# Spectral mixing and SiLU block on one Trainium2 core: x loads, evictions, filter loads and roundings of the ramp moved to other queues and places

## The chip, the core and the metric

The kernel runs on one core of one Trainium2 chip. The metric is the device time of one execution in microseconds (us). The engines are named as in the profile: PE (TensorE, matrix multiply; PEld is its weight load), DVE (VectorE), ACT (ScalarE), POOL (GpSimd) and SP (SyncE, which here only issues transfers). A name with a q, as SPq, is the queue of that engine, where DMA transfers are issued. Each engine executes its own instructions in the order in which the program emits them.

## What is computed

The input x is 8 x 3008 x 256 in float32. Each of the 256 channels is filtered along its 3008 positions in the frequency domain, and the result goes through a two-layer network with SiLU:

```python
X = np.fft.rfft(x, axis=1)
Y = X * (filt_r + 1j * filt_i)[None, :, :]
y = np.fft.irfft(Y, n=x.shape[1], axis=1)      # (8, 3008, 256)
h = y.reshape(24064, 256) @ w_in               # w_in 256 x 2048
g = h * (1.0 / (1.0 + np.exp(-h)))
out = g @ w_out                                # w_out 2048 x 256
```

The two filters are 1505 x 256 in float32. The weights come in as 64-bit floats and are turned into float32 on the chip.

## The kernel before

**Spectral part.** The transform of length 3008 is split into 47 x 64 and done with small matmuls. For one batch it runs in these pieces, all made by the function `spectral`:

- `load_x(u)`, u = 0 to 7, loads an eighth of x, `sums(u)` (DVE, line 292) adds and subtracts its two halves, and `stage1(u)` (PE, line 309) transforms it into two PSUM banks (`pa`). Two evictions by `evac` bring these to SBUF (`t1`), and two transfers issued by POOL (line 314) write them to a scratch tensor d1 in DRAM.
- `load_t2(g)`, g = 0 to 5, reads d1 back in another order (SP, line 383). `forward(g)` transforms (PE, `pb`, line 394), `multiply(g, k)` applies the filters (DVE, line 406), `add(g, k)` finishes the complex product (lines 414 and 415, on POOL in batch 0).
- `inverse(g)` (PE, `pc`), `even` (ACT) and `rows` (DVE, line 446) do the first half of the inverse transform, and `rows` writes to a second scratch tensor d2. `load_t4` reads that back (SP, line 456), `stage3(g)` ends the inverse (PE, `pd`, line 468), and two `evac` copies put each piece into y.

From batch 2 on, most of x is read in a folded form (`load_fold`, `fold`, `stage1_fold`, `evict_fold`), and `load_x`, `sums`, `stage1` are used for u = 6 and 7 only. Batch 1 uses them for all eight.

**Network.** `hidden(step)` and `project(step)` run 384 steps: 48 token groups times 8 pairs of hidden columns, so that a batch is 48 steps. A step's 14 matmuls with 128 x 128 weights (px, pyz, acc) fill PE, and DVE and ACT make the sums and SiLU between them. Each step has eight rounds.

**The ramp** is the straight code from line 777 on, before the first step. It loads x of batch 0, runs the spectral part of batch 0 up to four of its eight stage 3 pieces, and prepares the weights 0 to 8. Weights go in two functions: `weights(jp)` loads a pair of 64-bit blocks (`raw`, lines 711 and 714, on SP), and `rounded(j)` turns one block into float32 with DVE and ACT alternating (`work`, lines 724 to 732) and POOL multiplying the parts (`w_t`, line 737). After every odd j POOL also makes four sums of weights (shown at line 553). In the loop over groups the order is: forward, loads that belong to the group, multiply, add, the inverse of the group before, and at group 1 the roundings 2 and 3.

`load_filters(first, last)` loads the filters in 16 transfers on SP: the part for groups 0 and 1 before stage 1, the rest (groups 2 to 5) at group 0 of the loop, ahead of the raw weights of `weights(1)`. `evac` alternates between DVE (line 229) and ACT (line 231) by a flag.

**The planner.** Batches 1 to 7 are woven into the steps. `put(step, round, piece)` queues a piece for a step and round, counted from the batch's own first step `at`, so negative numbers lie in the batch before. Pieces are emitted in the order of their times by `until`. What is due before step 0 is emitted ahead of the first hidden step. The output stores (line 679, on SP) are queued in the same list: for the first token group of a batch they are due at steps 10.125 and 10.625 of the batch. The t2 loads of the next batch's groups 0 and 1, at `at - 37`, are due at step 11.0, and the t4 load that belongs to stage 3 piece 4 at step 10.375.

Of the kernel before, what the change touches and what calls it, by code (L numbers as in the profile page):

```python
# [52 lines left out]
B, S, C = 8, 3008, 256  # L53
DFF = 2048
N1, N2 = 47, 64
NS, NG = 24, 6
# [18 lines left out]
def slot_residue(g, bank, j):  # L75

    s = 2 * g + bank
    return (s, 47 - s, s + 12, 35 - s)[j]
# [77 lines left out]
def kernel(  # L156
# [9 lines left out]
    nc = tc.nc  # L166
# [42 lines left out]
    x_all = xpool.tile([128, 2, 2, 2 * C], FP32)  # L209
    x_t = [x_all[:, i] for i in range(2)]  # L210

    def load_filters(first, last):

        for j in (0, 2, 1, 3):
            s0, tau = slot_residue(0, 0, j), (1 if j % 2 == 0 else -1)
            for half in range(2):
                off, t = (s0, tau) if half == 0 else (94 - s0, -tau)
                for k, filt in enumerate((filt_r, filt_i)):
                    nc.sync.dma_start(  # L219
                        out=f_t[k][32 * j + half:32 * j + 32:2].rearrange("p g k c -> p (g k) c")[:, first:last],  # L220
                        in_=bass.AP(tensor=filt.tensor, offset=filt.offset + (off + t * first) * C,
                                    ap=[[94 * C, 16], [t * C, last - first], [1, C]]))

    flip = [0]

    def evac(dst, src):
        flip[0] ^= 1
        if flip[0]:
            nc.vector.tensor_copy(out=dst, in_=src)  # L229
        else:  # L230
            nc.scalar.copy(out=dst, in_=src)

    y = {}
    early = [0]

    def bank(b, name, spare=None):

# [11 lines left out]
    def spectral(b):  # L249
# [3 lines left out]
        xs, us, t2s, banks, prods, halves, t4s = {}, {}, {}, {}, {}, {}, {}  # L253

        def load_x(u):


            queue = nc.sync
            if b == 0:
                queue = (nc.sync, nc.scalar)[u % 2]  # L260
                if u == 0:
                    us["t1"] = gpool.tile([128, 2, 2, 2, C], FP32, name="t1_g", tag="g")
                if u in (0, 2):
                    xs["y"] = ypool.tile([128, 2, HALF], FP32, name=f"x_{b}_{u}", tag="y")
                if u < 4:
                    xs[u] = xs["y"][:, u % 2, 0:1024].rearrange("p (a n) -> p a n", a=2)
                elif u < 6:
                    xs[u] = t4pool.tile([128, 2, 2 * C], FP32, name=f"x_{b}_{u}", tag="t4")
                else:
                    xs[u] = x_t[u % 2]  # L270
                (nc.vector, nc.gpsimd)[u % 2].memset(xs[u][32:64], 0.0)
            else:
                xs[u] = x_t[u % 2]

            for r0 in range(3):
                for h in (range(2) if u % 2 == 0 else (1, 0)):
                    queue.dma_start(  # L277
                        out=xs[u][64 * h + r0:64 * h + N1:3],
                        in_=bass.AP(tensor=x.tensor,
                                    offset=x.offset + (b * S + 32 * r0 + 4 * u + 2 * h) * C,  # L280
                                    ap=[[3 * 32 * C, (N1 + 2 - r0) // 3], [32 * N1 * C, 2], [1, 2 * C]]))

        def sums(u):
            if b > 0 or u % 3 == 0:
# [174 lines left out]
        def stage3(g):  # L459
# [17 lines left out]
            for h in range(2):  # L477
# [4 lines left out]
                    load_t2=load_t2, forward=forward, multiply=multiply, add=add, inverse=inverse, even=even, rows=rows, load_t4=load_t4, stage3=stage3)  # L482
# [3 lines left out]
    def put(step, rnd, piece, *args):  # L486

        pending.append((step + rnd / ROUNDS, len(pending), lambda: piece(*args)))

    def plan(b, part):  # L490

        at = STEPS * b

        if b == 1:
            put(at - 51, 0, part["load_x"], 0)
            put(at - 51, 0, part["load_x"], 1)
            for u in range(8):
                put(at + u - (48 if u else 49), 5, part["sums"], u)
                put(at + u - 47, 3, part["stage1"], u)
        else:  # L500
            put(at - 72, 0, part["reverse_x"])
            for f, step, load, places in ((0, -56, -66, ((-60, 3), (-60, 5), (-59, 5), (-58, 5))),
                                          (1, -48, -55, ((-52, 3), (-52, 5), (-51, 5), (-50, 5))),
                                          (2, -40, -44, ((-42, 5), (-41, 3), (-41, 5), (-40, 3)))):
                put(at + load, 0, part["load_fold"], f)
                for k, (fold_step, rnd) in enumerate(places):
                    put(at + fold_step, rnd, part["fold"], f, k)

                put(at + step, 7, part["stage1_fold"], f)
                put(at + step, 7, part["evict_fold"], f, 0)  # L510
                put(at + step + 1, 0, part["evict_fold"], f, 1)
                put(at + step + 1, 5, part["evict_fold"], f, 2)
                put(at + step + 1, 5, part["evict_fold"], f, 3)
            for u, step in ((6, -46), (7, -45)):
                put(at - 47, 0, part["load_x"], u)
                put(at + step, 5, part["sums"], u)
                put(at + step + 1, 3, part["stage1"], u)
        put(at - 37, 0, part["load_t2"], 0)
        put(at - 37, 0, part["load_t2"], 1)
        for g, places in enumerate((  # L520
# [6 lines left out]
            pieces = (("forward", g), ("multiply", g, 0), ("multiply", g, 1), ("add", g, 0), ("add", g, 1))  # L527
            for (step, rnd), (piece, *args) in zip(places, pieces):
                put(at + step, rnd, part[piece], *args)
        for g, step in ((0, -32), (2, -24), (4, -16)):  # L530
            put(at + step, 7, part["inverse"], g, 2)
            put(at + step, 7, part["even"], g, 0, 2)
            put(at + step + 1, 0, part["even"], g, 1, 2)
            put(at + step + 1, 5, part["rows"], g, 0, 2)
            put(at + step + 2, 3, part["rows"], g, 1, 2)
        put(at - 14, 5, part["load_t4"], 0)
        put(at - 14, 5, part["load_t4"], 1)
        for g, step in enumerate((-11, -9, -6, -3)):
            put(at + step, 3, part["stage3"], g)
        plan_rest(b, part)  # L540

    def plan_rest(b, part):

        for g, (step, rnd) in enumerate(((10, 3), (11, 3), (16, 3), (18, 6))):
            put(STEPS * b + step, rnd, part["stage3"], 4 + g)
# [197 lines left out]
    def load_exact(j):  # L743
        for k in range(2):
            nc.sync.dma_start(out=places(j, 0)[:, k],
                              in_=moe_w_in[128 * k:128 * k + 128, 128 * j:128 * j + 128])
            nc.sync.dma_start(out=places(j, 1)[:, k].rearrange("p (q i) -> p q i", q=4),
                              in_=columns(moe_w_out[128 * j:128 * j + 128, :], 1)[:, k])
        if j % 2:
            combine_weights(j // 2)  # L750
# [9 lines left out]
    def weights(jp):  # L760
        if wide:
            load_weights(jp)

    def rounded(j):
        if wide:
            round_weights(j)
        else:
            load_exact(j)

    def inverse_rows(part, g):  # L770
        part["inverse"](g)
        for i in range(2):
            part["even"](g, i)
            part["rows"](g, i)
# [5 lines left out]
    part = spectral(0)  # L780
# [1 line left out]
        part["load_x"](u)  # L782
    nc.sync.dma_start(out=d_t, in_=d_dram.ap())
    weights(0)
    load_filters(0, 4)
    for u in range(3):
        part["sums"](u)
    for u in range(8):
        part["stage1"](u)
        if u + 3 < 8:  # L790
            part["sums"](u + 3)
    part["load_t2"](0)
    part["load_t2"](1)
    nc.sync.dma_start(out=e_t, in_=e_dram.ap())
# [2 lines left out]
    for g in range(NG):  # L797
        part["forward"](g)
        if g == 0:
            load_filters(4, 2 * NG)  # L800
            nc.sync.dma_start(out=wi_t, in_=wi_dram.ap())
            nc.sync.dma_start(out=wq_t, in_=wq_dram.ap())
        if g < 3:
            weights(1 + g)
        for k in range(2):
            part["multiply"](g, k)
        for k in range(2):
            part["add"](g, k)
        if g > 0:
            inverse_rows(part, g - 1)  # L810
        if g == 1:
            rounded(2)
            rounded(3)
    inverse_rows(part, NG - 1)
    weights(4)
    part["load_t4"](0)
# [78 lines left out]
```

## Time and profile before

| | value |
|---|---|
| time, median of 3 runs | 2656.36 us (2656.26 to 2659.49) |
| the profiled execution | 2659.17 us, span 2657.4 us |
| mean granted PE clock | 0.985 |
| PE busy in 0:20, 20:40, 40:60, 60:80, 80:100, 100:120, 120:140 us | 8.0, 8.8, 11.6, 2.1, 14.7, 6.7, 11.1 us of 20 |
| share of the DMA engines in the same stretches | 0.54, 0.92, 0.78, 0.87, 0.63, 0.69, 0.41 |
| x issues of batch 0 | SP 2.07 to 20.55 us, ACT 0.91 to 21.65 us |
| last write of d1 issued by POOL | 34.83 us |
| first matmul of the first step (px, line 582) | 124.84 us |

Times within the execution count from the start of the span. In a line of the timeline the first two numbers are the start and the length in us, then come engine, line, operation, what it writes and reads, and how many instructions were merged. In brackets stands how long the engine was idle before, and what ended that. The ramp ends at about 125 us, and the steps take about 6.55 us each from then on, longer at first.

The chain that ended last, over the whole span, is nearly all PE:

```profile
PE 92%; DVE 2%; SPq 2%; DMA 2%; issue 1%; ACT 0%; POOL 0%; DVEq 0%; ACTq 0%; POOLq 0%
```

### The profile page before, as it was taken

The numbers are of one execution on the slowest core, as the hardware profiler recorded it, in microseconds if no ns is written. First come the engines' busy times: TensorE is split into PE (matmuls) and PEld (weight loads), VectorE is DVE, ScalarE is ACT, GpSimd is POOL, SyncE is SP. The second block draws the span as 40 slices with busy tenths as digits, with TensorE's granted clock in tenths as the row PEclk, the third lists the DMA queues.
The fourth block names the chain that finished last, engine by engine and source line by source line (L and its number), as shares of the span: only waits on it lengthen the run. The fifth ranks groups of instructions, "written<-read, shape, count | busy, mean of one in ns | idle before, by whom it ended". The sixth has DMA issues, their size and how long they took to land.

```text
span 2657.4 us, 48231 instructions
## 1 busy us (share of the span) xinstructions
PE 2559.0 (96%) x18720; PEld 2162.9 (81%) x18720; DVE 1725.0 (65%) x3590; ACT 1096.3 (41%) x3000; POOL 482.7 (18%) x726
## 2 busy tenths in 40 slices
PE   4489999999999999999999999999999999999998
PEld 1268888888888888888888888888888888888987
DVE  4786666667666676666666676666766666555554
ACT  1244444444444444444444444444444444444443
POOL 3441111311121112111211111131112111100100
PEclk9599999999999999999999999999999999999999
DMA  7632222232223212331232222223222321211000
GB/s 214 189 105 64 71 65 57 63 74 72 59 69 70 62 61 71 76 68 42 69 75 62 65 72 64 56 67 71 66 65 69 74 57 28 55 22 21 9 16 16
DMA packets 207275, 176.11 MB, mean 66 GB/s; under 512 B 123812, under 2 KB 178852, under 8 KB 206644
## 3 DMA queue, kind: packets, MB, share of 16 engines
q1 hardware_dynamic: 185952, 120.91, 19.5%
q0 software_dynamic: 17296, 47.47, 5.6%
q10 hardware_dynamic: 3800, 4.67, 0.6%
q8 instruction: 147, 2.41, 0.4%
q14 instruction: 80, 0.66, 0.1%
HBM read 97.97 MB, written 84.41 MB: 69 GB/s over the span
## 4 chain that ended last, share of the span: by engine, by line
PE 92%; DVE 2%; SPq 2%; DMA 2%; issue 1%; ACT 0%; POOL 0%; DVEq 0%; ACTq 0%; POOLq 0%
PE acc L641 42%; PE px L582 25%; PE pyz L582 18%; PE pd L468 2%; PE pb L394 2%; PE pc L427 2%; SPq L277 1%; DMA t<-d 1%; PE pf L364 1%; PE pa L309 1%; DMA raw<-in_moe_w_out_dram 0%; SPq L219 0%; DVE g L553 0%; DVE u L292 0%; SPq L679 0%
## 5 line engine op out<-in xcount | busy, mean ns | idle before, releaser
L641 PE MATMUL acc<-g,w_t 128*128 128x256 f32 (+1 forms) x5376 | 1512.6, 375 | 0.4 <-DVE g L553 0.4
L641 PEld LDWEIGHTS acc<-g,w_t 128*128 128x128 f32 x5376 | 1022.1, 190 | 116.0 <-DVE g L553 0.8
L553 DVE TENSOR_TENSOR g<-pyz,abc 128x256 f32<-128x256 f32 (+1 forms) x1152 | 479.4, 416 | 542.4 <-ACT abc L603 301.3
L553 DVE TENSOR_TENSOR g<-g 128x256 f32<-128x256 f32 (+3 forms) x1152 | 619.4, 538 | 196.8 <-ACT g L586 183.6
L582 PE MATMUL px<-ty,w_t 128*128 128x256 f32 (+1 forms) x2304 | 688.0, 380 | 3.9 <-ACT abc L597 3.4
L586 ACT ACTIVATE g<-g 128x256 f32<-128x256 f32 (+1 forms) x1152 | 472.9, 410 | 247.1 <-DVE g L553 247.1
L553 POOL TENSOR_TENSOR s<-s 128x256 f32<-128x256 f32 (+1 forms) x329 | 259.7, 806 | 1455.8 <-DVE s L659 1444.8
L582 PEld LDWEIGHTS px<-ty,w_t 128*128 128x128 f32 x2304 | 424.2, 190 | 89.1 <-issue 31.5
L582 PE MATMUL pyz<-y,w_t 128*128 128x256 f32 (+1 forms) x1536 | 454.6, 378 | 1.7 <-DVE g L553 1.7
L582 PEld LDWEIGHTS pyz<-y,w_t 128*128 128x128 f32 x1536 | 284.1, 190 | 47.7 <-DVE g L553 7.2
L597 ACT COPY abc<-px 128x256 f32<-128x256 f32 (+1 forms) x384 | 141.5, 369 | 366.5 <-PE px L582 366.5
L603 ACT COPY abc<-px 128x256 f32<-128x256 f32 (+1 forms) x384 | 143.9, 375 | 317.3 <-PE px L582 317.0
L586 ACT ACTIVATE g<-px 128x256 f32<-128x256 f32 (+1 forms) x384 | 146.1, 380 | 307.7 <-PE px L582 307.7
L582 PE MATMUL px<-y,w_t 128*128 128x256 f32 (+1 forms) x768 | 230.6, 382 | 3.6 <-ACT g L586 2.7
L582 PE MATMUL pyz<-ty,w_t 128*128 128x256 f32 (+1 forms) x768 | 225.8, 376 | 5.0 <-DVE g L553 5.0
L582 PEld LDWEIGHTS px<-y,w_t 128*128 128x128 f32 x768 | 142.3, 190 | 43.0 <-ACT g L586 15.4
L582 PEld LDWEIGHTS pyz<-ty,w_t 128*128 128x128 f32 x768 | 145.9, 190 | 22.5 <-DVE g L553 6.2
L590 ACT COPY abc<-px 128x256 f32<-128x256 f32 (+1 forms) x384 | 135.3, 352 | 2.7 <-PE px L582 1.3
L229 DVE COPY y<-pd 128x376 f32<-128x376 f32 x64 | 51.2, 805 | 98.4 <-PE pd L468 98.4
L394 PE MATMUL pb<-t,d_t 64*32 64x256 f32 x1536 | 63.0, 407 | 38.8 <-DVE p L406 20.4
L468 PEld LDWEIGHTS pd<-wi_t,t 48*64 48x64 f32 x4096 | 69.4, 140 | 36.9 <-issue 25.1
L468 PE MATMUL pd<-wi_t,t 48*64 48x47 f32 x4096 | 77.6, 239 | 16.1 <-issue 8.4
(67 smaller groups left out, 1339.4 us busy)
## 6 DMA issues: line engine op xcount, KB each, us to landing
t<-d SPq DMA_DIRECT2D x96, 256.0 KB
t<-d SPq DMA_DIRECT2D x128, 192.0 KB
d<-q POOLq DMA_DIRECT2D x85, 256.0 KB, 2.6
out_dram<-o SPq DMA_DIRECT2D x636, 32.0 KB
d<-tf POOLq DMA_DIRECT2D x144, 96.0 KB, 2.6
d<-t POOLq DMA_DIRECT2D x52, 192.0 KB, 3.1
xr<-in_x_dram SPq DMA_DIRECT2D x6, 1472.0 KB
x_all<-in_x_dram SPq DMA_DIRECT2D x72, 96.0 KB
```

The source lines that it names most:

```text
L229: nc.vector.tensor_copy(out=dst, in_=src)
L277: queue.dma_start(out=xs[u][64 * h + r0:64 * h + N1:3], in_=bass.AP(tensor=x.tensor, offset=x.offset + (b * S + 32 * r0 + 4 * u + 2 * h) * ...
L394: nc.tensor.matmul(out=ps[k][32 * j:32 * j + 32, ri, :], lhsT=d_t[rows, 4 * g + at, ri, :], rhs=t2[rows, at, :], start=True, stop=True)
L427: nc.tensor.matmul(out=ps[j][64 * k:64 * k + 64, a, :], lhsT=e_t[rows, g + a, k, ri, :], rhs=zs[k][rows, ri, :], start=(a == 0 and ri == 0 ...
L468: nc.tensor.matmul(out=ps[h][c0:c0 + 64, cb, i, :], lhsT=t4s[g][rows, i, 128 * cb + c0:128 * cb + c0 + 64], rhs=wi_t[rows, :], start=True, ...
L553: eng.tensor_tensor(out=out, in0=in0, in1=in1, op=op)
L582: nc.tensor.matmul(out=out, lhsT=w_t[:, c, 0, jp], rhs=rhs, start=start, stop=True, skip_group_check=True)
L586: nc.scalar.activation(out=g[:, k, 0:n], in_=g[:, k, 0:n] if src is None else src, func=AFT.Silu)
L590: nc.scalar.copy(out=sums[:, 0, 0:n], in_=xo)
L597: nc.scalar.copy(out=sums[:, 1, 0:n], in_=xo)
L603: nc.scalar.copy(out=sums[:, 2, 0:n], in_=xo)
L641: nc.tensor.matmul(out=acc[pair][i][:, h, 0:n], lhsT=w_t[:, c, 1, jp], rhs=g[:, k, 0:n], start=(jp == 0 and h == 0), stop=last, skip_group ...
```

## The change

It has six edits, four in the ramp and two in the planner:

1. x of batch 0 is issued by SP alone and no longer by SP and ACT in turn (the choice of queue in `load_x` goes). Each u takes four transfers (rows 0 to 31 and 32 to 46 of each half) in place of six (every third row). The four-transfer form also holds for the later batches.
2. `evac` uses ACT alone as long as the ramp lasts (`early[0]` becomes None at its end), and alternates after it.
3. The second part of the filters is issued by POOL, after stage 1, and no longer by SP at group 0.
4. The rounding of weights 3 moves from group 1 to group 3.
5. The ahead-of-step-0 exception for `sums(0)` of batch 1 goes: it is due one step later, at step 0.625.
6. The t2 loads of groups 0 and 1 of the later batches are due one step earlier, at step 10.0.

```diff
-    def load_filters(first, last):
+    def load_filters(queue, first, last):
...
-                    nc.sync.dma_start(
+                    queue.dma_start(
...
-    flip = [0]
+    flip, early = [0], [0]
     def evac(dst, src):
         flip[0] ^= 1
-        if flip[0]:
+        if flip[0] and early[0] is None:
             nc.vector.tensor_copy(out=dst, in_=src)
         else:
             nc.scalar.copy(out=dst, in_=src)
...
-            queue = nc.sync
             if b == 0:
-                queue = (nc.sync, nc.scalar)[u % 2]
...
-            for r0 in range(3):
-                for h in (range(2) if u % 2 == 0 else (1, 0)):
-                    queue.dma_start(
-                        out=xs[u][64 * h + r0:64 * h + N1:3],
+            for h in range(2):
+                for r0, nr in ((0, 32), (32, N1 - 32)):
+                    nc.sync.dma_start(
+                        out=xs[u][64 * h + r0:64 * h + r0 + nr],
                         in_=bass.AP(tensor=x.tensor,
                                     offset=x.offset + (b * S + 32 * r0 + 4 * u + 2 * h) * C,
-                                    ap=[[3 * 32 * C, (N1 + 2 - r0) // 3], [32 * N1 * C, 2], [1, 2 * C]]))
+                                    ap=[[32 * C, nr], [32 * N1 * C, 2], [1, 2 * C]]))
...
-                put(at + u - (48 if u else 49), 5, part["sums"], u)
+                put(at + u - 48, 5, part["sums"], u)
...
-        put(at - 37, 0, part["load_t2"], 0)
-        put(at - 37, 0, part["load_t2"], 1)
+        put(at - 38, 0, part["load_t2"], 0)
+        put(at - 38, 0, part["load_t2"], 1)
...
-    load_filters(0, 4)
+    load_filters(nc.sync, 0, 4)
...
+    load_filters(nc.gpsimd, 4, 2 * NG)
     part["load_t2"](0)
...
         if g == 0:
-            load_filters(4, 2 * NG)
             nc.sync.dma_start(out=wi_t, in_=wi_dram.ap())
...
-        if g == 1:
-            rounded(2)
-            rounded(3)
+        if g in (1, 3):
+            rounded(2 + g // 2)
```

More of the change, by code (lines that the diff above doesn't have):

```diff
@@ L233 @@
     y = {}
-    early = [0]
     def bank(b, name, spare=None):
```

## The prediction

> **What bounds the kernel now.** I read the page's busy line first, then the table of stretches over the first 200 us, then the waits of each engine in the first 140 us, and last the timeline at the places that these named. All durations below are of the one profiled execution, whose span is 2657.4 us. Its own time is 2659.17 us, and the median of the three timed runs is 2656.36 us, so I carry the difference that I work out over to the median. About 5 us (0.2%) is what a measurement of this kernel can tell from no change.
>
> The page shows TensorE busy nearly throughout, and its slices show where it isn't.
>
> ```profile
> PE 2559.0 (96%) x18720; PEld 2162.9 (81%) x18720; DVE 1725.0 (65%) x3590; ACT 1096.3 (41%) x3000; POOL 482.7 (18%) x726
> ...
> PE   4489999999999999999999999999999999999998
> ```
>
> Each slice is 66 us. After the first two slices TensorE sets the pace, so an edit there pays only where it removes a hole on TensorE itself. In the first 140 us (the ramp: spectral part of batch 0 and the first half of the weights) TensorE is mostly idle, and there the chain runs through DMA, VectorE and the queues. The waits of the ramp, engine by engine (total us, times, longest us):
>
> ```profile
> DVE work L724 <- DMA raw<-in_moe_w_out_dram: 14.6, 1, 14.6
> ...
> DVE u L292 <- DMA x_all<-in_x_dram: 4.7, 1, 4.7
> ...
> PE pb L394 <- DVE p L406: 20.4, 1, 20.4
> ```
>
> VectorE executes in order. It stood 14.6 us for the second block of raw weights, and the multiply of group 2 was queued behind two roundings of those weights, so TensorE stood 20.4 us for the banks. The timeline shows the order (start, length, what):
>
> ```profile
> 40.39 2.78 SPq L383 DMA_DIRECT2D t<-d  x4
> ...
> 48.86 1.44 SPq L219 DMA_DIRECT2D filt<-in_filt_r_dram  x1
> ...
> 64.02 0.59 SPq L219 DMA_DIRECT2D filt<-in_filt_i_dram  x1
> ...
> 66.23 0.47 SPq L714 DMA_DIRECT2D raw<-in_moe_w_out_dram  x1
> ...
> 70.05 0.43 DVE L724 TENSOR_SCALAR work<-raw 128x512 uint32<-128x512 uint32 x1 [14.64 <-DMA raw<-in_moe_w_out_dram]
> ...
> 76.34 0.68 DVE L406 TENSOR_TENSOR z<-pb,filt 128x512 f32<-128x512 f32 x1
> ```
>
> The raw weights wait in SP's order behind the 16 filter transfers, which take SP from 48.86 to 64.6. A smaller hole of this kind lies at the seam to the steady loop, and another recurs once per batch:
>
> ```profile
> 131.09 1.29 DVE L292 TENSOR_TENSOR u<-x_all 111x512 f32<-111x512 f32 x2 [4.65 <-DMA x_all<-in_x_dram]
> 132.30 0.42 DVE L553 TENSOR_TENSOR g<-pyz,abc 128x256 f32<-128x256 f32 x1
> ...
> 132.77 1.22 PE L582 MATMUL pyz<-ty,w_t 128*128 128x256 f32 x2 [5.03 <-DVE g L553]
> ```
> ```profile
> 853.73 4.58 SPq L679 DMA_DIRECT2D out_dram<-o  x8
> 858.66 2.71 SPq L383 DMA_DIRECT2D t<-d  x4
> ...
> 861.55 0.59 PE L641 MATMUL acc<-g,w_t 128*128 128x256 f32 x2
> 862.45 0.59 PE L394 MATMUL pb<-t,d_t 64*32 64x256 f32 x2 [0.31 <-DMA t<-d]
> 864.17 1.09 PE L394 MATMUL pb<-t,d_t 64*32 64x256 f32 x30 [1.13 <-DMA t<-d]
> ```
>
> In the first, VectorE waits for x of batch 1 with the first hidden step's work behind it. In the second, the t2 loads come right after a block of output stores on SP, and TensorE reaches the forward transform before they have landed.
>
> **What the Trainium skill says.** "DMA: Bandwidth & Descriptors", section "Issuing engines are not separate DMA queues": transfers from every issuing engine run on the same 16 DMA engines, and issuing from several saves only sequencer time. The trace agrees: the DMA share is 0.91 to 1.05 from 24 to 36 us with three issuers at work. So I count the moved filter bytes in full. Same page, "Why a DMA increments its semaphore by 16 and not by 1": a transfer is spread over the largest number of engines up to 16 that divides the outer dimensions of both sides. Pieces of 32 and 15 rows give 16 and 15 engines, as 16 and 15 rows do now, so fewer transfers cost no spread. No run here shows that yet.
>
> **Part 1, the x loads and the evictions of stage 1.** Now 48 transfers for batch 0, 24 on SP (2.07 to 20.55) and 24 on ACT (0.91 to 21.65), about 0.78 us each. After, 32 on SP. SP's lone filter issues at 61.5 to 64.6 are 0.64 us apart, and its x issues of batch 1 have a median of 0.63 us, so I take 0.66: SP ends x at about 1.2 + 32 x 0.66 = 22.4 us, 1.8 us later than now (25 if they stay at 0.78, 21 at 0.62). Behind it on SP wait d_t, raw weights and 16 first filter transfers. In exchange ACT issues nothing, so that its first eviction need not wait until 21.69, which now holds the first write of d1 on POOL (16.2 us of wait, 22.58). All 16 evictions at 0.59 us on ACT are 9.4 us and fit beside x, which brings one u each 2.64 us. With 2.2 us to land, the last x is there at 24.7, its sums take 1.3, its matmuls 2.5, the evictions 1.2: d1 is written by about 34 us (now 38 to 39). But the t2 loads follow the first filters on SP, which end at 40.06 now and at 37 to 42 after. Net on the path to the first forward transform: 0, bounds -2 and +2.
>
> **Part 2, the second filters to POOL.** SP loses 16 issues, 15.8 us from 48.86 to 64.6. POOL gets 16 behind the last d1 write, from 30.5 on. POOL's d1 issues are 0.53 us each (8 in 4.27), so 8.5 us, until 39. Queued behind on POOL: the products and sums of weights 0 and 1 (1.66 + 1.42 + 2.88 = 6.0 us, until 45), then the first add, now at 48.91. It stays hidden. What SP issues next after t2 of group 2 (47.58, 1.24 us) is wi, wq and the second raw weights, four transfers in 1.9 us, so they are issued by about 52 and not 67.7. Can the DMA engines follow? Share times length of stretch up to the raw weights' landing at 70 sums to about 50 us of full DMA work. Up to 22 us some 15.5 of it can be done (x about 10.5, five eighths of the 7.7 that d1's 3.07 MB take at the 400 GB/s of 28 to 36 us, so 5). The other 34.5, if the engines then stay full, end at 56.5. I take 57 for the landing, bounds 52 and 63. VectorE is through with rows of group 0 at 55.4, so it waits 1 to 2 us and not 14.6.
>
> **Part 3, the roundings.** Two took 70.05 to 76.34; one is 2.9 to 3.0. So the multiply of group 2 starts at 57.1 + 3.0 = 60.1 and not 76.34: -16.2. The rounding put at group 3 adds its 3.4 us (72.92 to 76.34) there: +3.4, bounds 0 (hidden in VectorE's waits between groups) and +6, if POOL's 1.43 + 2.89 us for it hold the adds of group 4. They held those of group 2 now, so I charge nothing more. The ramp after that (five roundings, 101.48 to 121.07) is VectorE's and moves as a whole.
>
> **Part 4, stage 3's eight evictions on ACT.** Now VectorE takes four, from 120.99 behind the roundings, and the fourth stage 3 piece waits 2.15 us for a bank; the last eviction ends at 124.74. ACT is free at 118.6 and needs 0.70 us each: six by 122.8, the last piece's matmuls from 120.0 + 0.8 to 122.9, its two evictions to 124.3. -0.4, bounds -1.5 and +1.
>
> **Part 5, the first sums of batch 1 one step later.** The add of the first hidden step needs no x; it can run at 127 and not 132.3. The idle taken out is 4.65 us; the sums' own 1.29 us now lie within step 0, where VectorE has gaps of 0.78 and 1.71. By round 5 x is long there, in four transfers and not six. -4.3, bounds -5 and -2.
>
> **Part 6, t2 loads a step (6.55 us) earlier.** They pass ahead of the two blocks of output stores (8 transfers each, 4.2 and 4.6 us) and the t4 load. The last d1 write of batch 3 is issued at 846.19 and takes 2.6 us to land, so SP waits to about 849, and holds the stores by some 4 us; the next use of their buffers is nine steps away. t2 lands near 855, forward comes at 862. I measured from the start of the last acc pair to the next px pair: 3.33, 1.68, 3.64, 2.72, 1.55, 2.50, 1.76 us for batches 1 to 7. Against the 1.55 without a wait that is 1.78 + 0.13 + 2.09 + 1.17 + 0 + 0.95 + 0.21 = 6.3 us. -6.3, bounds -6.3 and 0.
>
> **Sum.** -16.2 + 3.4 - 0.4 - 4.3 - 6.3 = -23.8 us: span 2633.6, time 2656.36 - 23.8, about 2632.5 us.
>
> **The rivals.** *DMA-bound front* (0.24): with x, d1, raw weights and all filters in the first 45 us the t2 loads and raw weights get their turns late, or the rounding at group 3 costs its 6. The multiply of group 2 starts at 66, and the ramp gives -10.3 + 6 = -4.3; with -0.4, -4.3 and -4 from the rest -13: 2643. For it: shares of 1.05. Against it: 0.42 to 0.73 from 52 to 68, so there is room.
>
> *No gain in the ramp* (0.05): another wait of VectorE, for example on the adds of POOL, takes the place of the 14.6 us and only half of parts 5 and 6 remains, -5: 2651.
>
> *Slower* (0.05): POOL's filter issues stall. At p us each, the first add comes at 30.5 + 16p + 6, rows and one rounding follow 11.1 us later, and then 3.4. Parts 4 to 6 give 11 back, so the kernel gets slower once 16p exceeds about 37, p = 2.3 us. At p = 3 it is 2657 + 11, about 2668 us. For it: SP's own filter issues reached 1.88 us under a full DMA. Against it: no POOL issue in this ramp exceeds 0.62.
>
> **How the numbers follow.** The forecast has 0.66, with its own range 2624 to 2640 (landing at 52 to 63, the group 3 rounding at 0 to 6, t2 at half). To leave out no more than 2 in 10 I reach into the first rival: 2622 to 2645. Faster by over 0.2%: 0.92 (both first cases and part of the third); within: 0.04; slower: 0.04.
>
> **What would show it.** Right: the filter issues on POOL take 0.5 to 0.7 us each; the raw weights' wait before L724 shrinks to under 3 us; the multiply of group 2 starts near 60; the first px matmul comes near 111 to 113; VectorE's 4.65 us at the seam and TensorE's waits for t2 vanish. Wrong: the wait before L724 returns as one on POOL or on t2, or the d1 writes still end at 38.

## The result, and the profile after

| | before | after |
|---|---|---|
| time, median of 4 runs | 2656.31 us (2654.53 to 2659.49) | 2637.99 us (2635.87 to 2639.39) |
| ratio after to before | | 0.9929, 95% interval 0.9912 to 0.9946 |
| the profiled execution: time, span | 2659.17, 2657.4 us | 2635.87, 2633.7 us |
| first forward transform (`pb`) | 44.21 us | 45.48 us |
| multiply of group 2 starts | 76.34 | 63.22 |
| rows of the ramp end | 101.57 | 90.08 |
| first matmul of the first step (px) | 124.84 | 112.52 |
| first stage 1 matmul of batch 1 (`pa`) | 142.07 | 124.39 |

The kernel is 18.3 us faster by the medians (0.7%), 23.7 us by the two spans. The predicted 2632.5 us is 5.5 us too low, and the time lies within the range. Line numbers after the change are 3 lower from stage 1 on (line 403 is 406 of before).

The page after, busy time and PE's slices of 66 us: the second slice has gone from 4 to 6, the others stand.

```profile
PE 2559.7 (97%) x18720; PEld 2161.6 (82%) x18720; DVE 1716.9 (65%) x3578; ACT 1101.3 (42%) x3012; POOL 491.7 (19%) x742
...
PE   4689999999999999999999999999999999999998
```

VectorE's waits in the first 140 us after the change (total us, times, longest us):

```profile
DVE z L403 <- PE pb L391: 14.0, 1, 14.0
DVE q L443 <- ACT q L435: 7.8, 7, 2.7
DVE work L721 <- DMA raw<-in_moe_w_out_dram: 5.5, 1, 5.5
```

The 14.6 us for raw weights 2 are gone. The 5.5 us are those of weights 0, early in the ramp, and the 14.0 are the wait for the first forward transform (8.2 before). Of the rest, the seven waits for ACT's copy `q` will matter. TensorE's wait of 20.4 us for the banks of group 2 is gone as well, and its largest wait in the ramp is now the one for t2, which was 13.1 us before:

```profile
PE pb L391 <- DMA t<-d: 20.6, 3, 20.0
```

The timeline after, first the ramp and then the seam to the steps:

```profile
10.27 1.22 POOL L311 DMA_DIRECT2D d<-t  x2 [3.93 <-ACT t L232]
...
27.95 0.51 POOL L219 DMA_DIRECT2D filt<-in_filt_r_dram  x1
...
39.41 0.51 POOL L219 DMA_DIRECT2D filt<-in_filt_i_dram  x1 [0.17 <-issue]
...
53.92 0.47 SPq L711 DMA_DIRECT2D raw<-in_moe_w_out_dram  x1
...
57.72 0.34 ACTq L448 DMA_DIRECT2D d<-q  x1
...
58.51 0.88 DVE L443 TENSOR_TENSOR q<-q,pc 128x256 f32<-128x256 f32 x2 [2.71 <-ACT q L435]
59.30 0.42 DVE L721 TENSOR_SCALAR work<-raw 128x512 uint32<-128x512 uint32 x1
...
63.22 0.68 DVE L403 TENSOR_TENSOR z<-pb,filt 128x512 f32<-128x512 f32 x1
...
115.24 1.16 PE L579 MATMUL pyz<-ty,w_t 128*128 128x256 f32 x2
...
119.05 2.06 DVE L289 TENSOR_TENSOR u<-x_all 111x512 f32<-111x512 f32 x2
```

The first write of d1 is issued at 10.27 and not at 22.58. The filters' second part leaves POOL from 27.95 to 39.9, the raw weights are issued by 54.4 (before 67.7), and the rounding at 59.30 finds them there: no bracket stands behind it. The multiply of group 2 follows at 63.22. At the seam the second pair of pyz matmuls starts within the first step, without the 5.03 us of before, and the sums of batch 1 come after it.

**The difference, step by step.** The differences of the times in the table are -11.5 us at the end of rows, -12.3 at px (so -0.8 from the evictions of stage 3) and -17.7 at `pa` of batch 1 (-5.4 from the seam). Stage 3 piece 4 of batch 0, at 199 us, is still at -17.4 us. From there to the last batch the gap grows to -23.8 in steps of 0.0 to 2.1 us, one at the forward transforms of each later batch, which is -6.3 us. TensorE has no wait for t2 left after 200 us, where before it had six, 3.5 us in all.

### The profile page after: what moved, and what is told of

Its sections match the earlier page's. It is cut to its first block, busy times and chain, and to the rows that moved or that the text cites. A ratio compares the mean times of both kernels' runs of the same rounds, so it can differ in the third digit from the quotient of the medians.

```text
span 2633.7 us, 48160 instructions
## 1 busy us (share of the span) xinstructions
PE 2559.7 (97%) x18720; PEld 2161.6 (82%) x18720; DVE 1716.9 (65%) x3578; ACT 1101.3 (42%) x3012; POOL 491.7 (19%) x742
## 4 chain that ended last, share of the span: by engine, by line
PE 94%; DVE 3%; DMA 1%; issue 1%; ACT 1%; SPq 0%; POOL 0%; ACTq 0%; DVEq 0%; POOLq 0%
PE acc L638 42%; PE px L579 25%; PE pyz L579 18%; PE pd L465 2%; PE pb L391 2%; PE pc L424 2%; PE pf L361 1%; PE pa L306 1%; DVE g L550 1%; DVE u L289 0%; SPq L274 0%; DMA t<-d 0%; DVE work L726 0%; DMA filt<-in_filt_r_dram 0%; DVE work L721 0%
## 5 line engine op out<-in xcount | busy, mean ns | idle before, releaser
L232 ACT COPY y<-pd 128x376 f32<-128x376 f32 x68 | 53.9, 813 | 86.8 <-PE pd L465 86.8
```

## The experiments

In all of them "before" is the kernel before, run on the same chip. px stands for the start of the first px matmul, the end of the ramp. Two profiles of the changed kernel give px 112.52 and 113.79, and the three ramps with none of the ramp's edits (before, t2_alone, sums_alone) 123.5 to 124.8: about 1.3 us is not to be told from nothing in one profile.

| kernel | time us | before us | ratio, 95% interval | px us | multiply of group 2 |
|---|---|---|---|---|---|
| changed_again | 2637.20 | 2658.11 | 0.9922 (0.9910 to 0.9935) | 113.79 | 64.55 |
| t2_alone | 2652.35 | 2657.93 | 0.9977 (0.9970 to 0.9985) | 123.99 | 74.88 |
| sums_alone | 2652.74 | 2657.93 | 0.9980 (0.9972 to 0.9988) | 123.53 | 75.02 |
| f_filters_alone | 2657.13 | 2657.93 | 0.9997 (0.9989 to 1.0006) | 122.58 | 74.20 |
| u_filters_back | 2643.43 | 2657.93 | 0.9944 (0.9930 to 0.9958) | 120.74 | 69.27 |
| u_x_two_queues | 2643.33 | 2658.11 | 0.9942 (0.9927 to 0.9957) | 121.52 | 72.27 |
| u_evac_alternate | 2637.35 | 2658.11 | 0.9921 (0.9907 to 0.9935) | 114.58 | 64.49 |
| u_round_together | 2639.67 | 2658.11 | 0.9929 (0.9916 to 0.9943) | 115.76 | 68.28 |
| m_filters_later | 2643.51 | 2657.49 | 0.9950 (0.9933 to 0.9966) | 118.97 | 69.72 |
| m_filters_act | 2648.59 | 2657.49 | 0.9968 (0.9956 to 0.9979) | 124.99 | 75.71 |
| m_rows_pool | 2633.28 | 2657.49 | 0.9910 (0.9896 to 0.9925) | 111.04 | 61.66 |
| m_rows_pool_t2_first | 2634.65 | 2658.44 | 0.9911 (0.9894 to 0.9927) | 111.16 | 62.85 |

### The two planner edits, each alone

t2_alone is the kernel before with the t2 loads one step earlier:

```diff
-        put(at - 37, 0, part["load_t2"], 0)
-        put(at - 37, 0, part["load_t2"], 1)
+        put(at - 38, 0, part["load_t2"], 0)
+        put(at - 38, 0, part["load_t2"], 1)
```

> The kernel before, with one edit: t2 loads of groups 0 and 1 due at step 10.0. My theory: TensorE's waits at the first forward transform of batches 1 to 7 vanish, 6.3 us in sum; the ramp stays as it is to 0.3 us. Time -6 us (ratio 0.9977). Rival (SP waits for d1 and the output stores behind it come late, so that VectorE's transposes or the t4 load stall): waits of TensorE at pd or at the steps with transposes appear and the time is the same or longer.

Measured: 5.6 us by the medians, 7.3 by the spans, of which 0.85 are already there at px, where nothing was changed. So 6.4 us came from the steps. Each of the seven gaps that the prediction measured is 1.55 us here, and also in the changed kernel. What they hold above that is 6.3 us in the profile of before, but 5.2 and 5.4 us in f_filters_alone and sums_alone, whose t2 loads stand where they stood: the waits differ between executions, and the edit takes all of them. The timeline of t2_alone at the place that the prediction showed of before:

```profile
844.51 3.31 SPq L383 DMA_DIRECT2D t<-d  x4
847.92 4.33 SPq L679 DMA_DIRECT2D out_dram<-o  x8
```

The loads now go first. The output stores behind them are held by about 3 us; the list of waits after 200 us has none for a DMA any more, so nothing waited for them.

sums_alone is the kernel before without the exception for `sums(0)`:

```diff
-                put(at + u - (48 if u else 49), 5, part["sums"], u)
+                put(at + u - 48, 5, part["sums"], u)
```

> The kernel before, with one edit: the first sums of batch 1 are due at step 0.625. My theory: the 4.65 us for which VectorE waits for x ahead of the first hidden step vanish; the sums' own 1.3 us come back within the step in part: -4 to -5.4 us (ratio 0.9982), the first px matmul unchanged at 124.8, the first stage 1 matmul of batch 1 at 137 and not 142.1. Rival (x still late, so the wait only moves within step 0, or later x loads come late and VectorE waits at the next sums): -1 us or less.

Measured: 5.2 us by the medians. `pa` of batch 1 comes 6.4 us earlier and px 1.3 us, so the seam itself gave 5.1 us. Both planner edits came out as expected; they stand alone and need nothing of the ramp.

### The filters on POOL, alone and taken back

f_filters_alone is the kernel before with only the third edit:

```diff
+    load_filters(nc.gpsimd, 4, 2 * NG)
     part["load_t2"](0)
...
         if g == 0:
-            load_filters(4, 2 * NG)
```

> The kernel before, with one edit: the second part of the filters is issued by POOL after stage 1. My theory: the stall of VectorE on the second raw weights goes, since SP issues them some 15 us earlier. d1 is still written by 34.8, so POOL issues the filters until 43 and t2 lands some 3 us later than the 44 of before. Raw weights landed near 60, both roundings follow (6.3 us), the multiply of group 2 starts near 67 and not 76.3, the first px matmul comes at 115 to 116 and not 124.8: about -9.5 us in time. Rival, that the gain of the ramp comes mainly from the x loads and evictions of stage 1: -3 us or less, with the first px matmul after 121.

Measured: 0.8 us by the medians, with an interval that holds no change, and px at 122.58. The theory's 9.5 us did not come; what the rival named did. The timeline of f_filters_alone:

```profile
47.22 1.03 PE L394 MATMUL pb<-t,d_t 64*32 64x256 f32 x2 [16.11 <-DMA t<-d]
...
55.03 1.03 PE L394 MATMUL pb<-t,d_t 64*32 64x256 f32 x2 [2.75 <-DMA t<-d]
...
60.22 2.21 PE L427 MATMUL pc<-z,e_t 32*64 32x256 f32 x32 [1.31 <-DMA e_t<-e_tbl]
...
67.26 0.42 DVE L724 TENSOR_SCALAR work<-raw 128x512 uint32<-128x512 uint32 x1
```

The wait for raw weights 2 is gone here too (the rounding at 67.26 has none), but what stands ahead of it came later. The forward transforms of group 0 began at 47.22 and of group 1 at 55.03 (before, the first at 44.21, with no pause of over 0.3 us for t2 in the next two blocks), and the inverse waited for `e_t` until 60.2. POOL's 16 issues stretched from 35.63 to 48.74 us. So the moved bytes came in the way of t2 and `e_t`.

u_filters_back is the changed kernel with the filters on SP at group 0 again, and every other edit in place:

```diff
-    load_filters(nc.gpsimd, 4, 2 * NG)
     part["load_t2"](0)
...
         if g == 0:
+            load_filters(nc.sync, 4, 2 * NG)
```

> The changed kernel, with the second filters issued by SP at group 0 again. My theory: SP is held for 15 us again ahead of the raw weights, which land near 71; one rounding follows and the multiply of group 2 starts at 74 and not 63, the first px matmul near 123 and not 112.5: some 10 to 11 us slower than the changed kernel, about -13 against the kernel before. The t2 loads land 1 to 2 us earlier than in the changed kernel, since the filters are not in the DMA engines then, and nothing comes of it. Rival (x loads and evictions are the cause): no more than 4 us slower than the changed kernel.

Measured: px 120.74, with the old wait back (12.1 us for raw weights 2). By the gains over before it is 3.8 to 6.4 us slower than the changed kernel, less than the theory's 10 to 11. Against before, the filters alone move px by -2.3 us, everything else in the ramp by -4.1, and all together by -12.3 (-11.1 in the second profile). The two parts make 6.4 of these: about half of the ramp's gain comes only when both are there.

### What the filters need: x off ACT

u_x_two_queues is the changed kernel with `load_x` as before, on SP and ACT in turn and in six transfers:

```diff
+            queue = nc.sync
             if b == 0:
+                queue = (nc.sync, nc.scalar)[u % 2]
...
-            for h in range(2):
-                for r0, nr in ((0, 32), (32, N1 - 32)):
-                    nc.sync.dma_start(
...
+            for r0 in range(3):
+                for h in (range(2) if u % 2 == 0 else (1, 0)):
+                    queue.dma_start(
...
```

> The changed kernel with x loaded as before: SP and ACT in turn, six transfers for each u; evictions stay on ACT. My theory, after seeing that moving the filters alone brought 2 us: the front lives on d1 being written before the filters get into the DMA engines. ACT issues x until 21.7, its 16 evictions end near 31 and not 26.6, the last d1 write near 33.5 and not 28, POOL's filters start there and run into the t2 loads, the multiply of group 2 starts at 67 to 69, the first px matmul at 117 to 119: +5 to +7 us. Rival (the x edit pays nothing, the filters are enough once the rounding is split): first px matmul within 1.5 us of the changed kernel.

Measured: 6.1 us slower than changed_again on the same chip, as the theory had it, though px at 121.52 and the multiply of group 2 at 72.27 come later than it said. Its timeline shows where:

```profile
21.67 4.24 ACT L232 COPY t<-pa 128x512 f32<-128x512 f32 x8 [19.43 <-DMA x_all<-in_x_dram]
...
23.04 4.29 POOL L312 DMA_DIRECT2D d<-t  x8 [16.68 <-ACT t L232]
```

ACT makes no eviction before its own x issues have ended at 21.6, so POOL writes no d1 before 23.04. With x on SP alone the first write goes at 10.27. What that does to the DMA engines is seen in the stretches (columns: stretch, us, busy time of PE, PEld, DVE, ACT and POOL with instructions, granted clock, DMA share, GB/s). First the changed kernel, then f_filters_alone:

```profile
0.00:24.00 24.00, 16.45 (x62) 5.08 (x64) 14.06 (x21) 9.00 (x16) 12.05 (x22) 1.00 0.80 240
24.00:48.00 24.00, 3.54 (x33) 0.87 (x32) 5.00 (x10) 3.56 (x6) 16.02 (x28) 1.00 1.04 289
48.00:76.00 28.00, 20.37 (x278) 8.29 (x262) 19.50 (x39) 4.86 (x11) 12.47 (x19) 0.82 0.89 263
```

```profile
0.00:24.00 24.00, 9.73 (x34) 2.79 (x38) 12.99 (x20) 3.05 (x5) 7.15 (x13) 1.00 0.57 157
24.00:48.00 24.00, 7.89 (x36) 2.22 (x28) 10.57 (x19) 5.42 (x9) 15.29 (x29) 1.00 1.03 303
48.00:76.00 28.00, 12.87 (x161) 5.71 (x160) 14.15 (x26) 3.60 (x7) 14.90 (x22) 0.85 1.08 260
```

Share times length gives the busy time of the DMA engines. By 76 us it is the same in both: 19.2 + 25.0 + 24.9 = 69.1 us and 13.7 + 24.7 + 30.2 = 68.6 us. By 48 us it is 44.2 against 38.4. (Busy time is not bytes: GB/s times length gives 12.7 and 11.0 MB by 48 us, and 20.1 and 18.3 MB by 76.) Before, the three shares were 0.58, 0.92 and 0.77, and in u_x_two_queues 0.59, 1.00 and 1.06. So with x on two queues the engines stood idle for some 10 of the first 24 us, and that time could not be had back once they were full. The x edit fills 5 us of it, with d1 writes above all. The room that this makes is seen in u_filters_back, which has the x edit and not the filters on POOL:

```profile
24.00:48.00 24.00, 6.59 (x65) 2.30 (x72) 8.76 (x16) 3.67 (x6) 8.46 (x13) 1.00 0.73 236
```

From 24 to 48 us 6.5 us of DMA time are free there, and 2 were before. Into this room the filters go. Moved alone they only find full engines.

Edit 1 has two halves, the one queue and the four transfers in place of six. No run parts them, but the lengths of the issues say something (min/median/max in ns): first batch 0 of before, then batch 1 of before, which is on SP alone in the old form, then the first 24 issues of the changed kernel:

```profile
L277 ACTq DMA_DIRECT2D x<-in_x_dram x18: 597/632/1411, 0.9 to 16.2; - x18
L277 SPq DMA_DIRECT2D x<-in_x_dram x18: 592/700/961, 2.1 to 15.2; - x18
...
L277 SPq DMA_DIRECT2D x_all<-in_x_dram x48: 588/628/1475, 124.8 to 185.4; - x48
...
L274 SPq DMA_DIRECT2D x<-in_x_dram x24: 341/380/663, 1.1 to 12.2; - x24
```

An issue of the old form takes about as long on SP alone as beside ACT, and one of the new form is shorter: 0.38 us for these 24, 0.59 for the last eight of batch 0, and 0.43 for batch 1. At 0.63 us each the 48 issues of the old form would hold a lone SP for at least 30 us (an estimate from these lines), where the 32 of the new form took 17.3. So it seems to be the new form that lets SP do x alone. Why its issues are shorter is open.

### Evictions and roundings

u_evac_alternate is the changed kernel with the evictions shared as before:

```diff
-        if flip[0] and early[0] is None:
+        if flip[0]:
```

> The changed kernel with evictions alternating between VectorE and ACT in the ramp again. My theory: ACT is free of x issues, so stage 1 keeps pace with x either way and d1 ends within 0.7 us of 28; at the end of the ramp VectorE's four y copies come after the roundings again: first px matmul +0.5 to +1.5 us. Rival (ACT as the only evictor is what frees the front): +3 us or more.

Measured: 2637.35 us beside changed_again's 2637.20, no difference; px 0.8 us after the one and 2.1 after the other profile of the changed kernel. The stretch from the end of rows to px shows what the edit does: it takes 23.24 to 23.28 us in the five profiles in which VectorE shares the evictions, and 22.35 to 22.44 in the nine others. So it gives 0.9 us at the end of the ramp, too little for the medians to show. The first write of d1 is issued at 12.26, so even here it comes 10 us earlier than before. Freeing ACT of x issues did that, not giving it all evictions.

u_round_together is the changed kernel with both roundings at group 1:

```diff
-        if g in (1, 3):
-            rounded(2 + g // 2)
+        if g == 1:
+            rounded(2)
+            rounded(3)
```

> The changed kernel with roundings 2 and 3 both at group 1. My theory: VectorE's work is the same; the multiply of group 2 starts 3 us later (66.3), and the groups behind it run 1.5 to 3 us shorter: first px matmul 0 to +1.5 us. Rival (the split takes a wait off the path): +3 us or more.

Measured: px 2.0 us after changed_again's. The multiply of group 2 comes 3.7 us later (68.28 against 64.55), and from there to the end of rows it takes 25.1 us, the 25.2 of before; the changed kernel takes 26.9. So splitting the roundings wins 3.7 and costs 1.7. By the medians it is 2.5 us on the same chip, with intervals that overlap; px lies between the theory's 1.5 and the rival's 3 us.

### Who issues the filters, and when

If the filters only have to stay out of the way of t2, they can go later. m_filters_later is the changed kernel with POOL's call behind `rounded(1)`:

```diff
-    load_filters(nc.gpsimd, 4, 2 * NG)
     part["load_t2"](0)
...
     rounded(1)
+    load_filters(nc.gpsimd, 4, 2 * NG)
```

> The changed kernel with POOL's filter issues moved behind POOL's work for weights 0 and 1, ahead of the first adds. My theory is that the filters' bytes in the DMA engines ahead of t2 cost t2 its 3 us: the first forward transform starts at 42.4 to 43.5 and not 45.5 to 46. But POOL's issues (13 us where it has to wait for earlier transfers) now stand ahead of the first adds, so these come at 51 to 55: first px matmul 112 to 116, time the same as the changed kernel or up to 3 us more. Rival (t2 is late for another reason, as the first filters on SP): first forward stays at 45 or later.

Measured: 2643.51 us, px 118.97. The first forward came early as thought, at 42.17, but the gain did not follow. The timeline of m_filters_later:

```profile
54.45 0.51 POOL L219 DMA_DIRECT2D filt<-in_filt_i_dram  x1 [0.24 <-DMA filt<-in_filt_i_dram]
...
55.77 1.11 PE L424 MATMUL pc<-z,e_t 32*64 32x256 f32 x2 [6.29 <-POOL z L411]
```

POOL's issues, from 40.53 to 54.96, stood before its first adds, and the inverse waited for those. The first add came 4.6 us later than in the changed kernel, and the multiply of group 2 6.5 us later. The other 2 us stand at VectorE's wait for ACT's second copy `q`, 4.83 us here and 2.71 in the changed kernel. So the loss is above the theory's 3 us. If the issues stand in the way on POOL, another engine could make them. m_filters_act is m_filters_later with `nc.scalar` in place of `nc.gpsimd`:

```diff
-    load_filters(nc.gpsimd, 4, 2 * NG)
+    load_filters(nc.scalar, 4, 2 * NG)
```

> The changed kernel with the second filters issued by ACT after roundings 0 and 1. My theory: when the bytes go decides and not who issues them. ACT issues from 34 to about 45, where it has nothing else to do until 54; t2 lands at 44 to 46, POOL is free for weights and adds, so the multiply of group 2 starts within 2 us of the changed kernel's 63.2 to 64.6, first px matmul 111 to 114. Rival (POOL's own queue is what makes it work, a queue shared by order with other loads would hold them up): first px matmul after 117.

Measured: 2648.59 us; it is the slowest of the variants that keep every other edit. The timeline of m_filters_act:

```profile
32.83 0.62 ACTq L219 DMA_DIRECT2D filt<-in_filt_r_dram  x1
...
65.23 0.53 ACTq L219 DMA_DIRECT2D filt<-in_filt_i_dram  x1
65.81 0.37 ACT L435 COPY q<-pc 128x256 f32<-128x256 f32 x1 [32.26 <-DMA raw<-in_moe_w_in_dram]
66.21 0.88 DVE L443 TENSOR_TENSOR q<-q,pc 128x256 f32<-128x256 f32 x2 [11.30 <-ACT q L435]
```

Sixteen issues of about 0.6 us each took 33 us. The first six came 0.65 us apart; from 42 to 66 us, where the DMA share is 1.03, up to 8.8 us lie between the starts of two. ACT's next copy stood behind them, and VectorE 11.3 us behind that. "DMA: Bandwidth & Descriptors" of the Trainium skill, section "Issuing engines are not separate DMA queues", says that issuing from another engine saves sequencer time only. No run here contradicts that, as no choice of queue made room in the full stretch. But the engine that issues also pays for the stall, and that is the larger price. Why the same issues ended at 65.8 us on ACT and at 55.0 on POOL is open.

### The same stall, on ACT's d2 writes

The changed kernel has that stall too: ACT's d2 write (57.72 in the timeline above) was issued 1.9 us after its rows had ended, and VectorE stood 2.71 us for ACT's copy at 58.51 and 1.47 us more in the rounding, where it stood 0.84 and 0.42 us before. m_rows_pool is the changed kernel with all d2 writes of the ramp on POOL:

```diff
-                queue = nc.gpsimd if b > 0 or (g == NG - 1 and i == 0) else nc.scalar
-                queue.dma_start(out=d2[a0:a0 + 4].rearrange("a n h c -> (a n) h c"), in_=qt[:, a])
+                nc.gpsimd.dma_start(out=d2[a0:a0 + 4].rearrange("a n h c -> (a n) h c"), in_=qt[:, a])
```

> The changed kernel with all transfers to d2 in the ramp issued by POOL, as in the later batches, and not by ACT. In the changed kernel ACT stands at the first two of these issues for 1.9 and 1.1 us while the DMA engines are full, and VectorE waits behind it (2.7 and 1.5 us). My theory: these waits vanish, first px matmul 108.5 to 110.5, 3 to 4 us faster than the changed kernel. Rival (POOL has to wait in the same way and holds the adds[...]): no gain, or first px matmul later.

Measured: 2633.28 us (2632.79 to 2633.74), below every run of the changed kernel (the lowest is 2635.87), though on another chip than changed_again, and the two ratios' intervals overlap. It is the fastest here. px, at 111.04, is half a us after the theory's range. The timeline of m_rows_pool:

```profile
57.19 1.66 DVE L443 TENSOR_TENSOR q<-q,pc 128x256 f32<-128x256 f32 x4 [1.05 <-ACT q L435]
...
61.66 0.68 DVE L403 TENSOR_TENSOR z<-pb,filt 128x512 f32<-128x512 f32 x1
```

VectorE's wait for ACT has shrunk to 1.05 us, and rows run as a block of four. The multiply of group 2 starts at 61.66, though the first forward was 2.2 us later in this run than in the changed kernel (47.70). From the first multiply to that of group 2 it is 10.4 us, where the changed kernel takes 14.2.

m_rows_pool_t2_first is m_rows_pool with half of the first filters issued behind the t2 loads:

```diff
-    load_filters(nc.sync, 0, 4)
+    load_filters(nc.sync, 0, 4, (0, 2))
...
+    load_filters(nc.sync, 0, 4, (1, 3))
```

> The changed kernel with the d2 transfers of the ramp on POOL (as in the run before) and half of the first filters (8 of 16 transfers) moved behind the t2 loads on SP. My theory, the DMA engines being full from 12 us on, so that the order of bytes decides: t2 is issued when d1 has landed, at 33 to 35 and not 39 to 42, the first forward transform starts at 40 to 43, the second half of the first filters lands by 46, the multiply of group 0 starts at 45 to 47 and the raw weights come some 3 us earlier too: first px matmul 107.5 to 110, 2 to 4 us less than with the d2 edit alone. Rival (the bytes only change places, raw weights or POOL's adds still come when they came): first px matmul at 111 or later, same time as that run.

Measured: 2634.65 us, px 111.16: nothing gained, as the rival had it. The first forward comes at 41.57, 6.1 us earlier than in m_rows_pool, and the multiply of group 0 at 52.43, 1.2 us later. SP's eight remaining filter issues stretched from 38.1 to 50.6. The DMA share from 38 to 51 us is 0.96: with the engines so full the bytes only change places.

changed_again is the changed kernel itself, as it stands, run beside three of the others:

> The changed kernel itself, on the chip of the next three runs. Its profiled execution had the shortest time of its four and that of before one of the longest, so the two spans overstate the gain of 18.3 us in the medians. I expect the first px matmul at 112 to 113.5 again, and a ratio of 0.992 to 0.993, so a gain of 18 to 21 us; if it is 0.991 the 23.7 us of the two spans were right, and if 0.994 the parts add up to less than predicted.

It gave 2637.20 us and 20.9 us of gain by its medians.

## Why the prediction was right, and where it was not

The forecast of faster, and the size, were right: a span of 2633.6 us was worked out and 2633.7 measured. That closeness is partly luck. The terms were off in both directions, and the two profiled executions lie further apart than the medians. Of the signs that were named, the raw weights' wait, the 4.65 us at the seam and the waits for t2 are gone, POOL's filter issues take 0.49 to 0.61 us each, and px comes at 112.52. The multiply of group 2, at 63.22, is not near 60.

**Part 1, x and the evictions.** At the place where it was priced, the first forward transform, "net 0, bounds -2 and +2" held: +1.3 us. Its inner numbers were too cautious. SP issued 32 transfers from 1.15 to 18.47, 0.54 us each and not 0.66, since the 0.66 was read from filter issues and from x issues of the old form; and POOL was through with d1 at 27.95 and not at 30.5. (The upper end for 0.78 us each is 26.2 and not 25. And in the stretch from 24 to 36 us two engines issue, SP and POOL, not three: ACT's x issues ended at 21.65.) The t2 loads then lost what that won: they were issued at 38.91 and not 40.39, but took 6.6 us to the first matmul and not 3.8, since POOL's filters ran beside them (without these, u_filters_back begins at 42.42). The step that failed is to read "net 0 on the path" as the part's worth. Undone, it costs 6.1 us.

**Part 2, the filters.** SP's order put the raw weights' issue at 52 (measured 52.2 to 54.4). The sum of DMA work put their landing at 57; when the rounding came to them at 59.3 they were there. But the 16.2 us were worked out from this move and the split of the roundings, and the move alone gives 0.8 us of time. The working did use the early d1 writes of part 1 ("up to 22 us some 15.5 of it can be done"), and did not say that without them the term falls. POOL's issues end at 39.9 and not at 36.5, which 0.53 us each from 27.95 on would give, as some wait for earlier transfers. The wait named as hidden there did stay hidden.

**Part 3, the roundings.** The multiply of group 2 starts at 63.22 and not at 60.1, so -13.1 and not -16.2. What stands between is what the part did not see, VectorE's two waits for ACT behind ACT's d2 writes: 2.71 + 1.47 us, of which 2.9 are above what they were before. m_rows_pool takes the 2.9 away, and the time from the first multiply to that of group 2 falls by 3.8 us. At group 3 the second rounding costs 1.7 us and not 3.4, half of it hidden. Together -11.5 us at the end of rows, where the prediction has -12.8.

**Part 4.** -0.8 us in the two profiles and -0.9 over all of them, and not -0.4.

**Part 5.** -5.4 us (-5.1 alone) and not -4.3. The idle of 4.65 us went whole, and the sums' 1.29 us went into VectorE's gaps at no cost that shows.

**Part 6.** -6.3 us, as worked out from the seven gaps; alone -6.4. In that the profile of before was the one with the longest waits of three.

**From span to time.** Here the forecast lost most of its 5.5 us. The sum was set against the profiled execution before, 2659.17 us, near the top of its runs, and then taken from a median of 2656.36. The profiled execution after, 2635.87 us, is the lowest of its four. The two profiles differ by 23.3 us in time, the medians by 18.3 here and 20.9 in changed_again. The other profiles show that this pair lies wide apart. The end of rows is at 100.3 to 101.6 us in the three without the ramp's edits, and at 90.1 and 91.4 in the two of the changed kernel. From `pa` of batch 1 to the end it takes 2515.3 us in the profile of before, 2514.5 in f_filters_alone and in sums_alone, and 2508.9 to 2510.0 in the eleven profiles with edit 6. With the means of these, 0.9 for the evictions and 5.1 for the seam the gain is 21.7 us (an estimate). So about 2 us of the error are in the sum, which was read from an execution with long waits. The rest is where the medians lie. Why the kernel's runs differ by up to 5 us is open.

**The rivals.** The slower case needed POOL issues of 2.3 us each. They came 12.0 / 16 = 0.75 us apart in the changed kernel and 0.90 in m_filters_later, but 2.1 us on ACT, so its mechanism is real and lies near on another engine. The time of "DMA-bound front", 2643, is that of u_x_two_queues, 2643.33 us. Part of that is chance: the multiply of group 2 came at 72.27 there, and the rival had it at 66.

## What to carry to other kernels

When the DMA engines are full in a stretch, look at the stretch before it: idle DMA time there is what an earlier start can use. A transfer that was only moved into the full stretch gained 0.8 us here. Two edits to one such front should be priced together, and each undone in turn. Issue transfers that may stall from an engine whose next compute is not needed soon.

## What had not been expected

- The issues of an engine stretch, and hold its compute. ACT's 16 filter issues took 33 us (0.53 to 0.85 us of each is the issue itself), POOL's the same 16 between 10.9 and 14.4 us at a DMA share of 1.03 to 1.06. Full engines are not the whole of it: SP's same 16 took 15.7 us before, at a share of 0.65. What an issue waits for is not shown.
- The form of a transfer set the length of its issue, and a second queue did not change it much: 0.63 to 0.70 us in the old form, on two queues or one, and 0.38 to 0.59 in the new. For the same x, two queues needed 20.7 us with 48 issues and SP alone 17.3 with 32, and the second queue held ACT's evictions for 20 us.
- The share of the DMA engines reads up to 1.08 over 28 us, so a full stretch reads somewhat above 1.
